# Attention, Sinkhorn routing and a mixture of experts on one core: the steps of the later token groups placed anew in time, some vector work given to GpSimd, the first routing rows loaded ahead

## The chip, the cores and the metric

The kernel runs on one core of a Trainium2 chip. The metric is the device time of one execution in microseconds (us), the median of three runs. A core has TensorE (PE, matrix products, which write into banks of PSUM), VectorE (DVE), ScalarE (ACT), GpSimd (POOL) and SyncE (SP, which here issues nearly all transfers between HBM and SBUF). Each engine works through its own list of instructions in order; semaphores make one wait for another.

## What is computed

For 2304 tokens of width 512, with x from an attention layer over 4 x 8 heads (its code is left out: the change does not touch it):

```python
def _moe_ref(x, w_gate, w1, w2):
    N, D = x.shape                      # 2304, 512
    E = w_gate.shape[1]                 # 8; w1 [8,512,1024], w2 [8,1024,512]
    logits = x @ w_gate
    P = np.exp(logits - logits.max())
    for _ in range(8):
        P /= P.sum(1, keepdims=True) + 1e-09
        P /= P.sum(0, keepdims=True) + 1e-09
        P *= N / E
    out = np.zeros((N, D), dtype=np.float32)
    for e in range(E):
        h = np.maximum(x @ w1[e], 0.0)
        ye = h @ w2[e]
        out += P[:, e:e + 1] * ye
    return out
```

Every expert is applied to every token, weighted by its routing column.

## The kernel before

After attention and routing, `experts()` works in three groups of 768 tokens. Group 0 is scheduled by loops. It also makes the split weights (a high part and the rest, `w1h`/`w1l`, `w2h`/`w2l`) and stores them in HBM (`cache`), from which groups 1 and 2 load them again. Both products of an expert use Strassen-like schemes with seven block products: one item is a quarter of an expert's hidden width, with 384 columns (half of the group) at a time.

Groups 1 and 2 take up the first item alone and then 15 pairs of items. Each step (a matmul group, an addition, a load) is entered with `at(t, f, key)` at a planned time, to which the table `SHIFT` adds a number for the step's key; then all steps are sorted by time and written out in that order. So the table sets the order on each engine; when a step runs is decided on the chip by its semaphores. The letter ahead of a key's colon names the unit: `1f`/`2f` the item alone, `k` and `m` the middle pairs of group 1 (even, odd), `o` and `n` those of group 2 (even, odd), seven of each, `1l`/`2l` the last pair. Whether a step that either engine can do goes to VectorE (0) or GpSimd (1) is read from the table `ON` by `who`.

In a unit, TensorE makes per item the seven first products (line 1567) into PSUM banks `s_4107` to `s_4113`, `f_4110`; their weights come through a ring of seven tiles (`w1h0`, `w1l0`, `w1h1`, `w1l1` of the names below), loaded by SP at line 1557. VectorE adds the banks up into `temps` and `raw` (line 1546); at line 1595 it applies the maximum with 0 and the routing weight, whose rows lie in two tiles `pb`, loaded at line 1763 (the second is the tile that held `wo`). ACT copies the high parts into `xh` and `hb` (line 1588), VectorE or GpSimd subtract for the low parts `xl`, `hb`. The combinations of quarters (`temps<-temps,f` and the like) are operands of the 28 sums (line 1688), which TensorE adds into banks and VectorE into the tiles `m`. Their weights are raw rows (line 1726) combined by ACT and GpSimd, and kept operands loaded at line 1751 (`w2h`, `w2l`, `wu`, `w1l0`). Between group 1's first item and its sums TensorE also makes the last second products of group 0 (line 854). At the end of a group the sums are transposed (line 1799) and added to the partial result `ydr` (loaded at line 1786, added at line 1807).

SP issues each transfer only when the one eight before it has landed. In its rows below, `DMAHW` names one of these eight, and `PE`, `Pool`, `DVE` the engines it waits for.

Of the kernel before, what the change touches and what calls it, by code (L numbers as in the profile page):

```python
# [17 lines left out]
def kernel(  # L18
# [872 lines left out]
    def experts():  # L891
# [324 lines left out]
        with tc.manual_schedule(engines={mybir.EngineType.Activation, mybir.EngineType.DVE}):  # L1216
            for q in range(NI):
# [30 lines left out]
                for f in pieces:  # L1248
# [4 lines left out]
                    n = len(late)  # L1253
# [57 lines left out]
        def open_late():  # L1311
# [587 lines left out]
        now = 0.0  # L1899
# [86 lines left out]
```

## Time and profile before

| | |
|---|---|
| three runs, median | 1741.79 us (1741.28 to 1742.5) |
| profiled execution | 1740.03 us |
| its span in the trace | 1738.2 us |
| TensorE busy | 1687.8 us (97%) |
| VectorE busy | 1400.4 us (81%) |
| GpSimd busy | 968.2 us (56%) |
| ACT busy | 695.7 us (40%) |

Groups 1 and 2 take the span from about 751 us to its end. TensorE is busy nearly all the time, so what can be saved without leaving out work is its waits. A busy share of TensorE also contains matmuls at the lower of its two clock levels (granted clock 0.50 is 1.2 GHz, 1.00 is 2.4 GHz).

### The profile page before, as it was taken

The numbers are of one execution on the slowest core, as the hardware profiler recorded it, in microseconds if no ns is written. First come the engines' busy times: TensorE is split into PE (matmuls) and PEld (weight loads), VectorE is DVE, ScalarE is ACT, GpSimd is POOL, SyncE is SP. The second block draws the span as 40 slices with busy tenths as digits, with TensorE's granted clock in tenths as the row PEclk, the third lists the DMA queues.
The fourth block names the chain that finished last, engine by engine and source line by source line (L and its number), as shares of the span: only waits on it lengthen the run. The fifth ranks groups of instructions, "written<-read, shape, count | busy, mean of one in ns | idle before, by whom it ended". The sixth has DMA issues, their size and how long they took to land.

```text
span 1738.2 us, 29930 instructions
## 1 busy us (share of the span) xinstructions
PE 1687.8 (97%) x9803; PEld 1556.7 (90%) x9803; DVE 1400.4 (81%) x2884; ACT 695.7 (40%) x1736; POOL 968.2 (56%) x1020
## 2 busy tenths in 40 slices
PE   7999999999999999989999999999899999999998
PEld 6777879889998889979999999999899999999997
DVE  8877747777777777767989889899988888787888
ACT  7877743333333343323333333333233333333331
POOL 5755544577777877755454555454544444444443
PEclk9999999999999999999999999999999999999999
DMA  5444334578888788597768777876676676675654
GB/s 136 100 108 110 86 116 143 187 228 262 271 269 266 242 269 266 187 297 245 266 218 305 223 260 230 272 244 211 212 238 224 188 242 209 193 245 185 227 187 152
DMA packets 311851, 370.23 MB, mean 213 GB/s; under 512 B 81280, under 2 KB 191120, under 8 KB 311696
## 3 DMA queue, kind: packets, MB, share of 16 engines
q1 hardware_dynamic: 309776, 367.49, 66.6%
q8 instruction: 79, 1.29, 0.3%
q10 hardware_dynamic: 1920, 0.82, 0.2%
q14 instruction: 76, 0.62, 0.1%
HBM read 260.59 MB, written 107.63 MB: 212 GB/s over the span
## 4 chain that ended last, share of the span: by engine, by line
PE 74%; DVE 17%; DMA 4%; issue 2%; ACT 1%; POOL 1%; SPq 0%; DVEq 0%; ACTq 0%; POOLq 0%
PE s L1688 15%; PE s L854 14%; PE s L1567 11%; PE s L1100 10%; DVE temps L1546 5%; PE f L1567 4%; PE f L1100 3%; PE sx L1688 3%; PE x L648 2%; DVE raw L1546 2%; DVE temps L1595 2%; PE s L408 2%; DVE xl L1546 2%; DVE m L1546 1%; PE s L489 1%
## 5 line engine op out<-in xcount | busy, mean ns | idle before, releaser
L1546 DVE TENSOR_TENSOR temps<-s,temps 128x384 f32<-128x384 f32 x270 | 144.9, 551 | 82.9 <-ACT w1h L1745 29.4
L1032 POOL TENSOR_TENSOR w1l<-raw,w1h 128x512 fp32r<-128x512 f32 x85 | 117.3, 1393 | 117.0 <-ACT w1h L1031 83.0
L1174 DVE SCALAR_TENSOR_TENSOR acc<-s,P,acc 128x512 f32<-128x512 f32 x168 | 123.0, 744 | 37.5 <-PE s L854 37.0
L854 PE MATMUL s<-w2h,hhh 128*128 128x512 f32 x372 | 147.0, 395 | 0.7 <-DVE acc L1174 0.7
L854 PE MATMUL s<-w2h,hhl 128*128 128x512 f32 x372 | 146.1, 393 | 0.0
L854 PE MATMUL s<-w2l,hhh 128*128 128x512 f32 x372 | 146.1, 393 | 0.0
L1546 DVE TENSOR_TENSOR m<-s,m 128x384 f32<-128x384 f32 x240 | 122.4, 549 | 11.8 <-PE s L1688 11.6
L1595 DVE SCALAR_TENSOR_TENSOR temps<-temps,pb 128x384 f32<-128x384 f32 x180 | 118.0, 672 | 8.6 <-DMA pb<-pd 7.6
L1588 ACT CAST xh<-temps 128x384 fp32r<-128x384 f32 x128 | 64.7, 513 | 140.5 <-DVE temps L1595 91.9
L1131 DVE TENSOR_TENSOR temps<-s,temps 128x384 f32<-128x384 f32 x132 | 71.6, 554 | 51.5 <-PE s L1100 36.4
L1567 PE MATMUL s<-xh,w1h 128*128 128x384 f32 x388 | 108.7, 335 | 0.0
L1567 PE MATMUL s<-th,w1l 128*128 128x384 f32 x364 | 104.5, 334 | 0.1
L1567 PE MATMUL s<-th,w1h 128*128 128x384 f32 x356 | 102.6, 335 | 0.1
L1065 POOL TENSOR_TENSOR w2l<-raw,w2h 128x512 fp32r<-128x512 f32 x62 | 98.0, 1598 | 2.0 <-ACT w2h L1064 2.0
L1688 PE MATMUL s<-hb,w1l 128*128 128x384 f32 x338 | 81.6, 337 | 5.2 <-ACT hb L1588 3.5
L854 PEld LDWEIGHTS s<-w2h,hhh 128*128 128x128 f32 x372 | 70.4, 189 | 17.8 <-DVE acc L1174 4.3
L854 PEld LDWEIGHTS s<-w2h,hhl 128*128 128x128 f32 x372 | 70.2, 189 | 15.0
L1546 POOL TENSOR_TENSOR xl<-raw,xh 128x384 fp32r<-128x384 f32 x39 | 44.3, 1137 | 68.8 <-ACT xh L1588 68.8
L854 PEld LDWEIGHTS s<-w2l,hhh 128*128 128x128 f32 x372 | 70.3, 189 | 13.6
L1084 ACT ACTIVATE hhh<-temps 128x384 fp32r<-128x384 f32 x100 | 52.5, 525 | 73.3 <-DVE temps L1131 71.6
L1085 DVE SCALAR_TENSOR_TENSOR hhl<-temps,hhh 128x384 fp32r<-128x384 f32 x100 | 81.0, 810 | 0.0
L1588 ACT CAST hb<-temps 128x384 fp32r<-128x384 f32 x90 | 44.8, 513 | 79.9 <-DVE temps L1595 75.7
(392 smaller groups left out, 5653.9 us busy)
## 6 DMA issues: line engine op xcount, KB each, us to landing
w1h<-cache SPq DMA_DIRECT2D x245, 256.0 KB
w1l<-cache SPq DMA_DIRECT2D x243, 256.0 KB
raw<-in_moe_w_dram SPq DMA_DIRECT2D x156, 256.0 KB
cache<-w1h SPq DMA_DIRECT2D x27, 896.0 KB
cache<-w1l SPq DMA_DIRECT2D x27, 896.0 KB
w2h<-cache SPq DMA_DIRECT2D x64, 256.0 KB
w2l<-cache SPq DMA_DIRECT2D x32, 256.0 KB
cache<-raw SPq DMA_DIRECT2D x32, 256.0 KB
```

The costliest lines, as they stand in the source:

```text
L854: nc.tensor.matmul(out=pt, lhsT=h_[:, f, cols], rhs=w[:, f], start=(n == 0), stop=(n == 5))
L1032: tt(out=wl[:, i:i + 2], in0=src, in1=f32(wh[:, i:i + 2]), op=ALU.subtract)
L1065: nc.gpsimd.tensor_tensor(out=wl[:, j], in0=raws[j], in1=f32(wh[:, j]), op=ALU.subtract)
L1085: late.append(lambda: nc.vector.scalar_tensor_tensor(out=hl[:, f, c], in0=src, scalar=0.0, in1=f32(hh[:, f, c]), op0=ALU.max, op1=ALU.subt ...
L1100: nc.tensor.matmul(out=pt[:, 0:HT], lhsT=w[:, wi, k], rhs=x[:, k], start=(n == 0), stop=(n == total - 1),)
L1131: nc.vector.tensor_tensor(out=o, in0=x, in1=y, op=ALU.add)
L1174: nc.vector.scalar_tensor_tensor(out=acc[:, j], in0=pt, scalar=P[:, t_, e:e + 1], in1=acc[:, j], op0=ALU.mult, op1=ALU.add,)
L1546: return lambda: eng.tensor_tensor(out=now_(o), in0=now_(x), in1=now_(y), op=op)
L1567: pe.matmul(out=bank[:, 0:HT], lhsT=w[:, a, k], rhs=x[b][:, k], start=bool(first and n == 0), stop=bool(last and n == 5),)
L1588: at(t, lambda: ac.copy(out=hop[j][n][0], in_=src), f"{n}H{j}")
L1595: at(t, lambda: dv.scalar_tensor_tensor(out=dst, in0=src, scalar=0.0, in1=pb[int(n[2]) - 1], op0=ALU.max, op1=ALU.mult), f"{n}F{j}")
L1688: pe.matmul(out=bank[n, a][:, 0:HT], lhsT=w[p][:, 128 * a:128 * a + 128], rhs=x[r], start=(j == js[0] and i == 0 and (n, a) not in held), ...
```

## The change

Three things change, all in `experts()` for groups 1 and 2. Every number of `SHIFT` is another one (780 keys, and a new one for the weight loads of group 1's first item, `"1f:wl": 3.078`), which orders the steps anew. Twenty-nine entries of `ON` are turned: 19 to GpSimd, 10 to VectorE. GpSimd's list grows from 949 to 974 rows, and its combinations `temps<-temps,f` from 7 to 28; VectorE's shrinks from 2425 to 2398. The routing rows of group 1's first item are entered 8.5 in place of 2 units of time ahead.

```diff
         SHIFT = {
-            "1f:E20": 1.795, "1f:E21": 1.394, "1f:E30": 0.066, "1f:E31": -0.556, "1f:E40": 0.241,
...
-            "k:t4L1": 0, "o:t4L1": 1, "k:t1S0": 1, "o:t1S0": 1, "k:t1S1": 0, "o:t1S1": 0,
+            "k:t4L1": 0, "o:t4L1": 0, "k:t1S0": 1, "o:t1S0": 1, "k:t1S1": 0, "o:t1S1": 1,
             "k:t2S0": 0, "o:t2S0": 0, "k:t2S1": 0, "o:t2S1": 0, "k:t3S0": 0, "o:t3S0": 0,
-            "k:t3S1": 0, "o:t3S1": 0, "k:t4S0": 0, "o:t4S0": 0, "k:t4S1": 0, "o:t4S1": 0,
-            "k:s1S0": 1, "o:s1S0": 1, "k:s1S1": 0, "o:s1S1": 0, "k:s2S0": 0, "o:s2S0": 0,
-            "k:s2S1": 0, "o:s2S1": 1, "k:s3S0": 0, "o:s3S0": 0, "k:s3S1": 0, "o:s3S1": 0,
+            "k:t3S1": 0, "o:t3S1": 0, "k:t4S0": 0, "o:t4S0": 1, "k:t4S1": 1, "o:t4S1": 1,
+            "k:s1S0": 0, "o:s1S0": 0, "k:s1S1": 1, "o:s1S1": 1, "k:s2S0": 0, "o:s2S0": 1,
+            "k:s2S1": 1, "o:s2S1": 1, "k:s3S0": 0, "o:s3S0": 0, "k:s3S1": 1, "o:s3S1": 1,
...
                 if items[0][1] == 0 or u == 0:
-                    pb_load(now - (2.0 if u == 0 else 10.0), g, items[0][0])
+                    pb_load(now - (8.5 if u == 0 and g == 1 else 2.0 if u == 0 else 10.0), g, items[0][0])
```

Two lines more stand in the table, so line 1546 of before is line 1548 after, and so on.

Three places show what moves. The first is SP's list in front of group 1's first products, before. `cache_3918` holds the split weights of the first products, `pd` the routing rows, and `in_moe_w2_dram` the raw rows of w2.

```order
L1557 DMA w1h1_3904<-cache_3918 128x512 [waits DMAHW1_49,PE_49]
L1557 DMA w1h1_3904<-cache_3918 128x512 [waits DMAHW2_49,PE_49]
L1005 DMA cache_3918<-wo_8303 128x512 [waits DMAHW3_49,Pool_49]
L1557 DMA w1h1_3904<-cache_3918 128x512 [waits DMAHW4_49]
L1557 DMA w1l1_3905<-cache_3918 128x512 [waits DMAHW5_49]
L1557 DMA w1l1_3905<-cache_3918 128x512 [waits DMAHW6_49,PE_49]
L1557 DMA w1l1_3905<-cache_3918 128x512 [waits DMAHW7_49]
L1037 DMA cache_3918<-w1h0_3902 128x7x256 [waits DMAHW0_49]
L1037 DMA cache_3918<-w1l0_3903 128x7x256 [waits DMAHW1_49]
L1557 DMA w1h0_3902<-cache_3918 128x512 [waits DMAHW2_49,DMAHW0_49,PE_49]
L1763 DMA pb_8326<-pd_97 128x3x128 [waits DMAHW3_49,DVE_49]
L1763 DMA pb_8327<-pd_97 128x3x128 [waits DMAHW4_49]
```

The same place after.

```order
L1005 DMA cache_3918<-wo_8303 128x512 [waits DMAHW1_49,Pool_49]
L1765 DMA pb_8326<-pd_97 128x3x128 [waits DMAHW2_49,DVE_49]
L1765 DMA pb_8327<-pd_97 128x3x128 [waits DMAHW3_49,DMAHW1_49]
L1037 DMA cache_3918<-w1h0_3902 128x7x256 [waits DMAHW4_49]
L1037 DMA cache_3918<-w1l0_3903 128x7x256 [waits DMAHW5_49]
L1559 DMA w1h1_3904<-cache_3918 128x512 [waits DMAHW6_49,PE_49]
L1559 DMA w1h1_3904<-cache_3918 128x512 [waits DMAHW7_49,PE_49]
L1559 DMA w1h1_3904<-cache_3918 128x512 [waits DMAHW0_49]
L1559 DMA w1l1_3905<-cache_3918 128x512
L1559 DMA w1l1_3905<-cache_3918 128x512 [waits DMAHW2_49,PE_49]
L1559 DMA w1l1_3905<-cache_3918 128x512 [waits DMAHW3_49]
L1559 DMA w1h0_3902<-cache_3918 128x512 [waits DMAHW4_49,PE_49]
```

The two loads of `pb` and the two stores of 7 x 256 columns stood behind the first six weight loads; now all seven weight loads stand behind them. The second `pb` load waits for lane DMAHW1, which is the store of `wo` from the tile that it overwrites.

The second place is VectorE's list in a middle pair of group 2 (an `o` pair), from the first to the last read of bank `s_4108`, before.

```order
L1546 TENSOR_TENSOR temps_4098<-s_4108,temps_4098 128x384
L1546 TENSOR_TENSOR temps_4098<-temps_4098,f2_8325 128x384
L1546 TENSOR_TENSOR temps_4098<-s_4109,temps_4098 128x384
L1546 TENSOR_TENSOR temps_4098<-f_4110,temps_4098 128x384
L1595 SCALAR_TENSOR_TENSOR temps_4098<-temps_4098,pb_8326 128x384
L1546 TENSOR_TENSOR raw_8323<-s_4107,temps_4098 128x384
L1546 TENSOR_TENSOR temps_4098<-s_4108,temps_4098 128x384
L1546 TENSOR_TENSOR xl_68<-raw_8324,xh_67 128x384
L1595 SCALAR_TENSOR_TENSOR temps_4098<-temps_4098,pb_8327 128x384
L1595 SCALAR_TENSOR_TENSOR raw_8323<-raw_8323,pb_8327 128x384
L1546 TENSOR_TENSOR xl_68<-temps_4098,xh_67 128x384
L1546 TENSOR_TENSOR temps_4098<-s_4108,temps_4098 128x384
```

After, from the same first read on.

```order
L1548 TENSOR_TENSOR temps_4098<-s_4108,temps_4098 128x384
L1597 SCALAR_TENSOR_TENSOR temps_4098<-temps_4098,pb_8326 128x384
L1548 TENSOR_TENSOR temps_4098<-s_4109,temps_4098 128x384
L1548 TENSOR_TENSOR xl_68<-raw_8324,xh_67 128x384
L1548 TENSOR_TENSOR temps_4098<-f_4110,temps_4098 128x384
L1548 TENSOR_TENSOR raw_8323<-s_4107,temps_4098 128x384
L1548 TENSOR_TENSOR temps_4098<-s_4108,temps_4098 128x384
L1597 SCALAR_TENSOR_TENSOR temps_4098<-temps_4098,pb_8327 128x384
L1597 SCALAR_TENSOR_TENSOR raw_8323<-raw_8323,pb_8327 128x384
L1548 TENSOR_TENSOR xl_68<-temps_4098,xh_67 128x384
L1548 TENSOR_TENSOR temps_4098<-s_4108,temps_4098 128x384
```

`temps<-temps,f2` has left for GpSimd, and the multiplication by `pb_8326` and the subtraction into `xl` have moved ahead of the addition out of bank `f_4110`.

The third place is SP's list in an `n` pair of group 2, before. `cache2` holds raw rows of w2, `cache3` kept operands.

```order
L1726 DMA raw2_8328<-cache2_3919 128x512 [waits DMAHW6_49,Pool_49]
L1726 DMA raw2_8329<-cache2_3919 128x512 [waits DMAHW7_49,Pool_49]
L1751 DMA wu_8496<-cache3_3920 128x512 [waits DMAHW0_49]
L1557 DMA w1l1_3905<-cache_3918 128x512 [waits DMAHW1_49,PE_49]
L1557 DMA w1l1_3905<-cache_3918 128x512 [waits DMAHW2_49,PE_49]
L1557 DMA w1l1_3905<-cache_3918 128x512 [waits DMAHW3_49,PE_49]
L1557 DMA w1h0_3902<-cache_3918 128x512 [waits DMAHW4_49,PE_49]
L1751 DMA w1l0_3903<-cache3_3920 128x512 [waits DMAHW5_49]
L1557 DMA w1h1_3904<-cache_3918 128x512 [waits DMAHW6_49,PE_49]
```

After.

```order
L1728 DMA raw2_8328<-cache2_3919 128x512 [waits DMAHW5_49,Pool_49]
L1728 DMA raw2_8329<-cache2_3919 128x512 [waits DMAHW6_49,Pool_49]
L1753 DMA w1l0_3903<-cache3_3920 128x512 [waits DMAHW7_49]
L1559 DMA w1h1_3904<-cache_3918 128x512 [waits DMAHW0_49,PE_49]
L1559 DMA w1h1_3904<-cache_3918 128x512 [waits DMAHW1_49,PE_49]
L1559 DMA w1l1_3905<-cache_3918 128x512 [waits DMAHW2_49,PE_49]
L1559 DMA w1l1_3905<-cache_3918 128x512 [waits DMAHW3_49,PE_49]
L1559 DMA w1l1_3905<-cache_3918 128x512 [waits DMAHW4_49,PE_49]
L1559 DMA w1h0_3902<-cache_3918 128x512 [waits DMAHW5_49,PE_49]
```

The load of the kept operand into `w1l0_3903` stood behind `wu` and four weight loads; now it follows the raw rows directly, ahead of six weight loads.

## Rows read from the trace of the kernel before

**Rows 1.** The page's busy us (share of the span), instructions.

```profile
PE 1687.8 (97%) x9803; PEld 1556.7 (90%) x9803; DVE 1400.4 (81%) x2884; ACT 695.7 (40%) x1736; POOL 968.2 (56%) x1020
```

**Rows 2.** TensorE's waits, 751 to 790 us: total, times, longest.

```profile
PE f L1567 <- DMA w1h<-cache: 3.5, 1, 3.5
PE s L1688 <- POOL xl L1546: 1.1, 1, 1.1
PE s L854 <- DVE acc L1174: 0.7, 1, 0.7
```

**Rows 3.** TensorE's waits, 790 to 1270 us.

```profile
PE s L1688 <- ACT xh L1588: 4.4, 1, 4.4
PE s L1688 <- DMA w2h<-cache: 2.6, 2, 2.4
...
PE s L1688 <- DVE temps L1546: 1.5, 1, 1.5
```

**Rows 4.** TensorE's waits, 1270 to 1710 us.

```profile
PE s L1688 <- DVE temps L1546: 5.5, 14, 0.6
PE s L1688 <- ACT hb L1588: 3.5, 3, 1.3
PE s L1688 <- DMA w1l<-cache: 1.7, 2, 1.1
```

**Rows 5.** Windows: busy us (x) of PE, PEld, DVE, ACT, POOL; clock, DMA share, GB/s.

```profile
761.00:767.00 6.00, 5.62 (x15) 4.85 (x16) 1.03 (x2) 0.62 (x3) 2.12 (x3) 0.50 0.77 129
801.00:805.00 4.00, 4.00 (x16) 4.00 (x15) 4.00 (x10) 2.52 (x5) 0.01 (x1) 0.57 0.56 182
805.00:820.00 15.00, 15.00 (x88) 15.00 (x87) 7.98 (x16) 2.97 (x7) 7.16 (x9) 1.00 0.64 173
1100.00:1200.00 100.00, 99.10 (x558) 95.96 (x557) 90.70 (x181) 34.06 (x80) 51.65 (x55) 1.00 0.78 261
1500.00:1600.00 100.00, 96.42 (x546) 94.16 (x546) 84.11 (x157) 33.04 (x79) 41.97 (x46) 1.00 0.65 205
```

**Rows 6.** The chain that ended last, 740 to 1738 us: start, us, what.

```profile
750.60 7.53 DMA cache<-w1h
...
795.02 5.21 DMA w2h<-cache
...
1249.25 7.32 DMA m<-ydr
...
1465.17 5.55 DMA w1l<-cache
```

**Rows 7.** SP's timeline, 742 to 763 us: start, us, transfer.

```profile
758.62 0.91 SPq L1763 DMA_DIRECT2D pb<-pd  x2
```

**Rows 8.** TensorE's timeline, 751 to 775 us, idle before in brackets.

```profile
751.32 0.44 PE L1567 MATMUL s<-xh,w1h 128*128 128x384 f32 x1
...
761.38 0.69 PE L1567 MATMUL f<-th,w1h 128*128 128x384 f32 x1 [3.52 <-DMA w1h<-cache]
...
774.32 0.51 PE L1688 MATMUL s<-xh,w1l 128*128 128x384 f32 x2
```

**Rows 9.** Transfers: 40 slices of 742 to 768 us; packets, 761 to 763.

```profile
GB/s 83 336 320 351 342 350 342 334 200 367 325 299 268 344 407 381 328 337 380 388 381 391 386 383 386 386 312 291 181 40 67 65 37 63 74 97 229 347 403 407
...
DMA packets 219, 0.11 MB, mean 55 GB/s; under 512 B 6, under 2 KB 219, under 8 KB 219
```

**Rows 10.** VectorE's timeline, 1433 to 1440 us.

```profile
1437.91 1.21 DVE L1546 TENSOR_TENSOR temps<-s,temps 128x384 f32<-128x384 f32 x2
```

**Rows 11.** Groups of VectorE and GpSimd, 1300 to 1700 us: busy, mean ns.

```profile
L1546 DVE TENSOR_TENSOR temps<-s,temps 128x384 f32<-128x384 f32 x120 | 64.5, 551 | 56.3 <-PE s L1567 23.4 <-ACT w1h L1745 23.3 <-ACT w1l L1745 4.2
L1595 DVE SCALAR_TENSOR_TENSOR temps<-temps,pb 128x384 f32<-128x384 f32 x79 | 56.8, 740 | 0.5
...
L1546 DVE TENSOR_TENSOR temps<-temps,f 128x384 f32<-128x384 f32 x20 | 18.7, 933 | 0.0
...
L1546 POOL TENSOR_TENSOR temps<-temps,f 128x384 f32<-128x384 f32 x6 | 8.1, 1353 | 35.1 <-DVE hb L1546 35.1
```

More of the change, by code (lines that the diff above doesn't have):

```diff
@@ L1334, in experts @@
         SHIFT = {
[170 rows of a table removed]
[171 rows of a table added]
+            "o:wl": 2.927,
         }
```

358 rows, old and new, of tables (ON, SHIFT) are left out of this document.

## The prediction

> **What bounds the kernel now.** I read the page's busy shares first: TensorE works 97% of the span [rows 1]. Then the waits of TensorE by stage, since only they can be won back, then the stretches by window, then for each wait the chain that leads to it. The change leaves the order as it was up to the queue in front of 751 us, so the search is in 751 to 1738 us.
>
> The waits fall into three kinds. At the start of group 1 TensorE stands 3.5 us for one weight load and 1.1 us for a GpSimd subtraction [rows 2]. In the rest of group 1 and the turn to group 2 it stands 4.4 us for an ACT copy, 2.6 us for weight loads and 1.5 us for VectorE [rows 3]. In group 2 it stands 10.7 us in 19 short waits (5.5 + 3.5 + 1.7) [rows 4]. The windows say the same: 99.1% busy in a steady stretch of group 1, 96.4% in one of group 2, where VectorE is busy only 84% [rows 5]. So group 2 is limited by order, not by an engine's total work. The windows show one more cost: the granted clock is 0.50 (1.2 GHz) in 761 to 767 us, right after the 3.5 us stand, and 0.57 in 801 to 805 us, after the one at 800 us. Full pace is 88 matmuls in 15 us, 0.17 each; the 16 in 801 to 805 us would need 2.7 of the 4.0 us, so that stand cost another 1.3 us.
>
> **The sum, place by place.** It is made against the profiled execution, 1740.03 us, which lies 1.76 us below the median of the three runs.
>
> *Start of group 1 (a cost).* Before, SP issues the loads of weights for six products, then the two stores of 896 KB from 750.60 us on [rows 6], then the load of the last product, then the routing rows `pb` at 758.62 us [rows 7]. TensorE starts the first product at 751.32 us and the seventh, which waits for that last load, at 761.38 us [rows 8]. Now the routing rows and the stores go ahead of all seven loads, as the order shows. Does a load overtake what was issued before it? The first store landed 7.53 us after its issue [rows 6], at 758.13 us, though both stores together are 4.8 us of transfer (below): the loads issued ahead of them took the time between. So transfers are served in the order of issue, and the first product waits for everything ahead: the raw rows and `wo` (about 750 us by the old issue times, an estimate), the routing rows, the stores. The stores hold 2 x 896 KB = 1.84 MB, at the 381 to 391 GB/s of the slices before 759 us [rows 9] 4.8 us. The routing rows hold 2 x 192 KB = 0.39 MB and run at 55 GB/s in 761 to 763 us [rows 9], which would be 7.1 us and is the bound above; the slices of that stretch reach from 37 to 97 GB/s, near 65 on most, which is 6.0 us. I take 6 us. The first load lands about 1.5 us behind the last store (256 KB at 385 GB/s is 0.7 us, and a landing). Sum: 750 + 6 + 4.8 + 1.5, about 762 us, for the first product, in place of 751.3.
>
> From there: before, 12.94 us passed from the seventh product's start to the sums at 774.32 us, with the cold clock and a 0.7 us wait for VectorE in it [rows 2, 8]. Now seven products follow the stand; the six more are 36 matmuls, at 0.17 each 6.1 us. The cold stretch stays, since TensorE stands longer than before, and the 0.7 us goes. 762 + 12.9 + 6.1 - 0.7 = 780.3 us, 6 us later. Against that the GpSimd wait behind it goes, 1.1 us [rows 2]. **+5 us.** Bounds: if the stores do not hold up the loads, the first product starts near 755 us and the old stand is gone, about -2 us; if the second half of the routing rows (its tile is `wo`'s, so it waits for the landing of `wo`, which the order shows) leaves the queue empty for 2 us and the rows take 7.1 us, about +9 us with the landings.
>
> *800 us.* The third `w2h` load was issued at 795.02 us and landed 5.21 us later [rows 6]; TensorE stood 2.4 us [rows 3] and paid 1.3 us of cold clock. That load now stands ahead of two weight loads, some 6 us earlier in the plan, and TensorE comes later. **-3.5 us**, at least -1, at most -3.7.
>
> *Around 836 us* VectorE's 1.5 us [rows 3]: its additions are ordered anew. **-1 us** (0 to -1.5).
>
> *Turn to group 2, 1259 us.* The chain: the last load of `ydr` took 7.32 us, to 1256.57 us [rows 6]; VectorE's additions waited for it, and behind them in its order stood the combination that ACT copies for TensorE's next sum: the 4.4 us [rows 3]. In the order the combination now goes ahead of one of the three additions that were before it, and two of the four loads are issued earlier, but the last one hardly. Behind so long a stand the clock will have fallen as at 800 us, at the same 1.3 us (an estimate from that row). I take half of the two: **-3 us** (0 to -5.7).
>
> *Group 2, per pair.* In the seven `o` pairs TensorE waits up to 0.6 us [rows 4] for a bank that VectorE reads last at 1437.91 us [rows 10]. In its order there stood ten operations between the first and the last read of that bank, now nine, and the one that left is `temps<-temps,f`, 933 ns on average here [rows 11]. 0.93 is more than 0.6, so this wait should close. In the `n` pairs, 1.7 us [rows 4] go to waits that end when `w1l0` lands: issued at 1465.17 us, 5.55 us on the way [rows 6]. It is now issued ahead of six loads, which the old issues put some 3 us earlier, more than the longest wait of 1.3 us. The three waits under ACT's name (3.5 us [rows 4]) stand at the same sum; ACT's copy was early, so I count them with it. All 10.7 us closed, less some that comes back: **-9 us** (-4 to -10.7).
>
> *What the moved operations cost.* 21 of these combinations go from VectorE (933 ns) to GpSimd (1353 ns [rows 11]): its list has 7 before and 28 now. GpSimd is busy 42% here, so I cost it at nothing; a result that is needed at once comes 0.42 us later, and if it stands behind another operation of that kind, up to 1.8 us. Additions that read a bank take 551 ns, multiplications with both inputs in SBUF 740 ns on average at the same place [rows 11]: two-input operations stretch. The Trainium skill's page "SBUF — State Buffer", section "Who interferes with whom", says that a VectorE instruction with two SBUF inputs contends with GpSimd's reads, and one with a single SBUF input does not. By that rule GpSimd work beside additions out of PSUM is free, and this part would be -10.7 in place of -9; the 933 and 740 ns against 551 agree with it, but where the new GpSimd work lies in time no row shows.
>
> Sum: 5 - 3.5 - 1 - 3 - 9 = -11.5 us; the end of the kernel changes by 0, within 3 us. On the profiled execution 1728.5 us, on the median 1741.8 - 11.5 = **1730.3 us**.
>
> **The rivals.** *The start costs nothing.* If loads pass stores, or the routing rows are quick when nothing competes, the start is -2 us and the sum -18.5: 1723.3 us. For it: the queue was full here before, so no row shows a load behind stores alone; against it: the routing rows ran at 55 GB/s in a stretch in which no packet of 2 KB or more moved [rows 9]. As a mechanism, these rows would have to move at the pace of the other transfers, 0.39 MB at 385 GB/s in 1.0 us, which takes 5 us off the start: 1725.3 us. The Trainium skill's page "DMA: Bandwidth & Descriptors", section "Specifications", gives 512 bytes as the least transfer for line rate, and a row of `pb` is cut into 128 x 4 = 512 bytes; by it this would be the case, but the row of 55 GB/s speaks against it, and the measurement decides.
>
> *The group-2 waits only move.* `temps` comes earlier, and then the next operand (`xl`, `hb`) is the late one. Then group 2 gives 2 us in place of 9 and the turn nothing: +5 - 3.5 - 1 - 2 = -1.5, 1740.3 us. For it: in each pair several operands come within some tenths of each other; against it: VectorE has 16% idle.
>
> *GpSimd comes late (slower).* Place: the pairs of both groups, at the 21 combinations that went to GpSimd. Each later by 0.42 us plus half of another such operation, 0.68 us, gives 1.1 us, 23 for the 21: -11.5 + 23 = +11.5, 1753.3 us. It decides from 11.5/21 = 0.55 us each. For it: the steady pairs of group 1 have no slack on TensorE to give (99.1% busy), only to lose. Against it: GpSimd is half idle.
>
> *The start is dear.* With +9 there and all else as forecast the sum is 9 - 3.5 - 1 - 3 - 9 = -7.5, 1734.3 us; with a third of the turn and 5 us of group 2, -1.5, 1740.3 us.
>
> **Chances and range.** The forecast, 1726 to 1736 us, 0.50; the start costs nothing, 0.12, of this 0.03 by the page's rule; the waits only move, 0.17; GpSimd late, 0.13; the start dear, 0.08. A difference of 0.2%, 3.5 us, is about what a measurement of this kernel can tell from no change. Faster: the first two, a third of the third (0.06) and most of the last (0.06), 0.74. Same: most of the third, 0.10, with 0.04 of the others. Slower: 0.12. The range from 1722 to 1742 us leaves out most of the GpSimd case and a little below, under 2 in 10; the forecast's own range is 1726 to 1736.
>
> **What would show it.** Right: `pb` issued near 750 us, the first product of group 1 near 762 us with a cold clock behind it, the sums 4 to 7 us later than 774.3; no stand at 800 and less at 1259; in group 2 the waits for `temps`, `hb` and `w1l` under 3 us in all, TensorE above 98.5% in its windows. Wrong: a first product before 757 us or after 765; waits of TensorE for GpSimd's `xl`, `hb` or for ACT copies of what GpSimd made, above 0.3 us in each pair; TensorE under 98.5% in 900 to 1200 us.

## The result and the profile after

The changed kernel takes 1710.53 us (median of four runs, 1710.07 to 1712.3) against 1741.53 us for the kernel before in the same runs: ratio 0.9827, 95% interval 0.981 to 0.9845. The forecast was 1730.3 us in a range from 1722 to 1742. The direction was right; the size was not: 31 us instead of 11.5. The spans of the two profiled executions, 1738.2 and 1708.3 us, differ by 29.9 us.

The page's first part for the changed kernel answers to [rows 1].

```profile
PE 1669.9 (98%) x9803; PEld 1555.8 (91%) x9803; DVE 1354.1 (79%) x2845; ACT 696.8 (41%) x1736; POOL 1004.3 (59%) x1059
```

TensorE has the same 9803 matmuls in both pages, while VectorE's busy time fell by 46 us and GpSimd's grew by 36. That says little about the place. For this I set the start of the same work in both traces side by side, since TensorE makes its products in the same order in both. These are TensorE's timelines at six places, first the kernel before: the first product of the first pair of group 1, of the next two pairs, of the item alone that opens group 2, of the first pair of group 2, and the sums of group 2's last pair.

```profile
783.11 0.33 PE L1567 MATMUL s<-xh,w1h 128*128 128x384 f32 x1
...
816.54 0.33 PE L1567 MATMUL s<-xh,w1h 128*128 128x384 f32 x1
...
848.40 0.33 PE L1567 MATMUL s<-xh,w1h 128*128 128x384 f32 x1
...
1244.48 0.33 PE L1567 MATMUL s<-xh,w1h 128*128 128x384 f32 x1
...
1267.76 0.33 PE L1567 MATMUL f<-xh,w1h 128*128 128x384 f32 x1
...
1710.40 0.51 PE L1688 MATMUL s<-xh,w2h 128*128 128x384 f32 x2
```

The same places in the changed kernel, with three rows of the start of group 1 ahead of them (they answer to [rows 8]).

```profile
754.40 0.50 PE L854 MATMUL s<-w2h,hhh 128*128 128x512 f32 x1 [3.70 <-DVE acc L1174]
...
761.88 0.69 PE L1569 MATMUL s<-xh,w1h 128*128 128x384 f32 x1 [5.19 <-DMA w1h<-cache]
...
779.17 0.51 PE L1690 MATMUL s<-xh,w1l 128*128 128x384 f32 x2
...
786.68 0.33 PE L1569 MATMUL s<-xh,w1h 128*128 128x384 f32 x1
...
817.30 0.33 PE L1569 MATMUL s<-xh,w1h 128*128 128x384 f32 x1
...
846.85 0.33 PE L1569 MATMUL s<-xh,w1h 128*128 128x384 f32 x1
...
1232.09 0.33 PE L1569 MATMUL s<-xh,w1h 128*128 128x384 f32 x1
...
1255.38 0.33 PE L1569 MATMUL f<-xh,w1h 128*128 128x384 f32 x1
...
1679.48 0.51 PE L1690 MATMUL s<-xh,w2h 128*128 128x384 f32 x2
```

The lead of the changed kernel grows from -3.57 us at the first pair (it is late there) to -0.76, 1.55, 12.39, 12.38 and 30.92 us. The differences from place to place are what each stage cost or gave (minus is time gained; the turn holds group 2's item alone, with its products and sums):

| stage | forecast, us | measured, us |
|---|---|---|
| start of group 1, up to its first pair | +5 | +3.6 |
| first pair (the stand at 800) | -3.5 | -2.8 |
| second pair (around 836) | -1 | -2.3 |
| the other pairs of group 1 | 0 | -10.8 |
| turn to group 2 | -3 | 0.0 |
| pairs of group 2, up to the last sums | -9 | -18.5 |
| end | 0 | +1.0 |
| sum | -11.5 | -29.9 |

The measured column is from one trace of each kernel. A second trace of the changed kernel, from a run described below (span 1711.5 us), gives 4.3, -3.0, -2.0, -8.7, 0.0, -17.6 and 0.3 us, so the two large terms hold to about 2 us.

Where the gain arose, TensorE's windows are nearly full. The view by window of the changed kernel, with the columns of [rows 5]:

```profile
755.00:765.00 10.00, 4.81 (x15) 3.94 (x14) 1.42 (x3) 2.00 (x5) 2.18 (x3) 0.51 1.06 384
900.00:1000.00 100.00, 100.00 (x577) 99.55 (x576) 85.58 (x173) 35.15 (x83) 56.40 (x66) 1.00 0.80 264
1100.00:1200.00 100.00, 99.23 (x565) 97.26 (x565) 88.23 (x178) 35.02 (x82) 56.63 (x64) 1.00 0.75 244
1500.00:1600.00 100.00, 100.00 (x577) 99.35 (x576) 82.71 (x161) 35.28 (x85) 55.18 (x58) 1.00 0.71 233
```

577 matmuls of 384 columns in 100 us are 0.173 us each, the full pace; in 1500 to 1600 us there were 546 before [rows 5]. Between 1270 and 1680 us TensorE has no listed wait any more, where [rows 4] had 10.7 us in 19. In 790 to 1270 us the waits of TensorE are these three and four of 0.4 to 0.6 us each:

```profile
PE s L1690 <- DVE m L1809: 2.3, 1, 2.3
PE s L1569 <- DVE tl L1548: 1.4, 1, 1.4
PE s L1569 <- DMA w1h<-cache: 0.7, 2, 0.4
```

### The profile page after: what moved, and what is told of

The parts are those of the page before. It is cut to its first block, busy times and chain, and to the rows that moved or that the text cites. A ratio compares the mean times of both kernels' runs of the same rounds, so it can differ in the third digit from the quotient of the medians.

```text
span 1708.3 us, 29942 instructions
## 1 busy us (share of the span) xinstructions
PE 1669.9 (98%) x9803; PEld 1555.8 (91%) x9803; DVE 1354.1 (79%) x2845; ACT 696.8 (41%) x1736; POOL 1004.3 (59%) x1059
## 4 chain that ended last, share of the span: by engine, by line
PE 88%; DVE 6%; DMA 3%; ACT 1%; issue 1%; POOL 1%; SPq 0%; DVEq 0%; ACTq 0%; POOLq 0%
PE s L1690 19%; PE s L1569 18%; PE s L854 15%; PE s L1100 10%; PE f L1569 6%; PE sx L1690 4%; PE f L1100 3%; PE x L648 2%; PE s L408 2%; PE f L1690 2%; DMA w1h<-cache 2%; PE s L489 1%; DVE m L1548 1%; PE f L854 1%; PE f L833 1%; DVE temps L1548 1%
## 5 line engine op out<-in xcount | busy, mean ns | idle before, releaser
L1548 POOL TENSOR_TENSOR xl<-temps,xh 128x384 fp32r<-128x384 f32 x46 | 57.2, 1243 | 92.9 <-ACT xh L1590 92.9
L1597 DVE SCALAR_TENSOR_TENSOR temps<-temps,pb 128x384 f32<-128x384 f32 x180 | 102.9, 579 | 1.2
```

Source lines behind the costliest of these rows:

```text
L1548: return lambda: eng.tensor_tensor(out=now_(o), in0=now_(x), in1=now_(y), op=op)
L1597: at(t, lambda: dv.scalar_tensor_tensor(out=dst, in0=src, scalar=0.0, in1=pb[int(n[2]) - 1], op0=ALU.max, op1=ALU.mult), f"{n}F{j}")
```

## The experiments

Two theories. Theory 1: the order of the steps (the times) decides, and TensorE's waits cost more than the idle time that was shown. Theory 2: the relief of VectorE (the engines' table) decides. On the start of group 1 a third question stood by itself: does the new queue order cost what the sum said?

**The two tables apart.** First the times alone, that is the changed kernel with all 29 turned entries of `ON` as before:

```diff
-            "k:t3S1": 0, "o:t3S1": 0, "k:t4S0": 0, "o:t4S0": 1, "k:t4S1": 1, "o:t4S1": 1,
+            "k:t3S1": 0, "o:t3S1": 0, "k:t4S0": 0, "o:t4S0": 0, "k:t4S1": 0, "o:t4S1": 0,
...
```

> All numbers of the time table and the routing rows as in the changed kernel, but the table of engines as before. If the order of steps decides (theory 1), it stays within 4 us of the changed kernel, under 1715 us. If the relief of VectorE by 29 moved entries decides (theory 2), it goes back by more than half of the 31 us, over 1726 us.

Measured: 1740.12 us, ratio 0.9991 to the kernel before (0.9978 to 1.0004). Then the engines alone, the kernel before with the changed `ON` and nothing else:

```diff
-            "k:t3S1": 0, "o:t3S1": 0, "k:t4S0": 0, "o:t4S0": 0, "k:t4S1": 0, "o:t4S1": 0,
+            "k:t3S1": 0, "o:t3S1": 0, "k:t4S0": 0, "o:t4S0": 1, "k:t4S1": 1, "o:t4S1": 1,
...
```

> The kernel before with only the table of engines of the changed one. Theory 1 (order decides): 1736 us or more, it may be slower than before, since the times were placed for the other engines. Theory 2 (relief of VectorE decides): 1726 us or less.

Measured: 1738.61 us, 0.9975 (0.9962 to 0.9989). Each theory was to keep more than half of the gain; neither table alone gives more than about a seventh of it. By stage, the new times alone start the first pair 3.2 us late, as the changed kernel does (3.6); they gain 3.3 us in group 1 from the third pair on and nothing in the pairs of group 2. The new engines alone gain 0.4 and 3.5 us there. The waits of TensorE in the pairs of group 2 (1275 to 1680 us) show why. With the new times and the old engines:

```profile
PE s L1690 <- DVE temps L1548: 6.1, 13, 0.8
PE s L1690 <- DVE hb L1548: 2.1, 6, 0.4
```

With the old times and the new engines:

```profile
PE s L1688 <- DVE xl L1546: 4.6, 7, 0.9
PE s L1688 <- DMA w1l<-cache: 2.8, 3, 1.4
PE s L1688 <- ACT hb L1588: 0.9, 2, 0.6
```

In the one, VectorE still does the work for which the new order leaves no room; in the other, the loads and the subtractions stand where they stood. So both theories fall as stated: the times are placed for these engines, and only the two together take the waits away.

**Two entries of the 29.** The changed kernel with the t4 combinations of the `o` pairs back on VectorE:

```diff
-            "k:t3S1": 0, "o:t3S1": 0, "k:t4S0": 0, "o:t4S0": 1, "k:t4S1": 1, "o:t4S1": 1,
+            "k:t3S1": 0, "o:t3S1": 0, "k:t4S0": 0, "o:t4S0": 0, "k:t4S1": 1, "o:t4S1": 0,
```

> The changed kernel with two entries put back to VectorE, the combinations t4 of both items in the o pairs of group 2 (14 operations). Theory 2: VectorE's last read of the bank comes 0.9 us later in each of seven pairs, the wait of about 0.6 us in front of the fifth sum returns, and with what such a wait costs in TensorE's pace the run is 4 to 7 us slower, 1715 to 1717 us. Theory 1: under 1 us, since the order alone left room.

Measured: 1723.39 us (ratio 0.9887, 0.9864 to 0.991), 12.9 us above the changed kernel's median, or 10.4 by the two ratios: well above the 4 to 7 us expected. From the first product of group 2's first pair to the sums of its last, the place where the two entries act, its trace takes 436.0 us and the changed kernel's 424.1. The waits of TensorE from 1270 to 1680 us and a window of it:

```profile
PE s L1690 <- DVE hb L1548: 6.4, 7, 0.9
PE s L1690 <- DVE temps L1548: 0.3, 2, 0.2
```

```profile
1300.00:1400.00 100.00, 97.86 (x556) 95.80 (x555) 83.25 (x161) 33.33 (x78) 43.28 (x46) 1.00 0.67 220
```

The waits shown are 6.7 us; the time lost in the pairs is 11.9. The window shows the same: 2.1 us idle, but 20 matmuls fewer than the 576 which the changed kernel has in 1300 to 1400 us, and 20 x 0.173 = 3.5 us. So the time lost is more than the idle time listed, here nearly twice as much.

**Four entries of group 1.**

```diff
-            "k:s1S0": 0, "o:s1S0": 0, "k:s1S1": 1, "o:s1S1": 1, "k:s2S0": 0, "o:s2S0": 1,
-            "k:s2S1": 1, "o:s2S1": 1, "k:s3S0": 0, "o:s3S0": 0, "k:s3S1": 1, "o:s3S1": 1,
-            "k:s4S0": 1, "o:s4S0": 1, "k:s4S1": 1, "o:s4S1": 0,
+            "k:s1S0": 0, "o:s1S0": 0, "k:s1S1": 0, "o:s1S1": 1, "k:s2S0": 0, "o:s2S0": 1,
+            "k:s2S1": 0, "o:s2S1": 1, "k:s3S0": 0, "o:s3S0": 0, "k:s3S1": 0, "o:s3S1": 1,
+            "k:s4S0": 1, "o:s4S0": 1, "k:s4S1": 0, "o:s4S1": 0,
```

> The changed kernel with four entries put back to VectorE: the raw sums s1 to s4 of the second item in the k pairs of group 1 (28 operations of 256 columns, about 0.4 us each). If the 10.8 us of group 1's steady pairs come from order that is fitted to these entries, each of seven pairs gets waits back: 1714 to 1722 us. If VectorE's 11% of idle time takes them up, under 1.5 us more than the changed kernel.

Measured: 1713.44 us (0.9837, 0.982 to 0.9854), 1.9 us above the changed kernel on the same chip (1711.55 us, below), between the two expectations and nearer the second; the intervals of the two ratios nearly coincide. From the third pair to the last of group 1 its trace takes 385.7 us, where the two traces of the changed kernel take 385.2 and 387.4. So VectorE takes these 28 operations up, and not every entry of the table matters as the two above do.

**The groups apart.** The kernel before with the changed numbers and engines of the units `2f`, `o`, `n` and `2l` alone, and the changed kernel with these as before. Some 400 entries of the tables differ in each; here is one line of the first:

```diff
...
-            "k:s2S1": 0, "o:s2S1": 1, "k:s3S0": 0, "o:s3S0": 0, "k:s3S1": 0, "o:s3S1": 0,
+            "k:s2S1": 0, "o:s2S1": 1, "k:s3S0": 0, "o:s3S0": 0, "k:s3S1": 0, "o:s3S1": 1,
...
```

> The kernel before with the times and engines of the changed one for the units of group 2 alone (2f, o, n, 2l). Aligned by unit, the two traces differ by 18.5 us between the first and the last sums of group 2. If these 18.5 us are group 2's own, this runs at 1742 - 18.5 = 1723 us, within 3; if they hang on what group 1 hands over, it stays above 1730 us.

> The changed kernel with the times and engines of group 2's units (2f, o, n, 2l) as before. Group 2 alone gave 20 us of 31. If the groups add up, this keeps 11 us: 1728 to 1733 us. If they lean on each other, the two parts miss the 31 us by more than 4.

Measured: 1721.4 us (0.9874, 0.9852 to 0.9896) and 1730.23 us (0.9942, 0.9923 to 0.9961). That is 20.1 and 11.4 us below the kernel before in the same runs, 31.5 together, and the whole change gave 31: the groups add up, and two thirds of the gain are group 2's own. The traces agree stage by stage. With group 2 alone changed, its pairs take 424.9 us (442.6 before, 424.1 changed) and group 1 from the third pair on 395.0 (396.1 and 385.2); with group 1 alone changed it is 442.8 and 384.8.

**The start of group 1.** The changed line alone, in the kernel before:

```diff
-                    pb_load(now - (2.0 if u == 0 else 10.0), g, items[0][0])
+                    pb_load(now - (8.5 if u == 0 and g == 1 else 2.0 if u == 0 else 10.0), g, items[0][0])
```

> The kernel before with the one changed line alone: the routing rows of group 1's first item go ahead of the two stores and the seventh weight load, behind the first six. By the reading that transfers are served in the order of issue, the seventh product comes about 6 us later, while VectorE no longer waits for the rows: 0 to 5 us slower than before, 1742 to 1747 us. If the rows were what holds group 1 up, it would be 2 to 5 us faster.

Measured: 1740.59 us, 0.9998 (0.9985 to 1.0011), no difference. The wait for the seventh load grew from 3.5 to 5.4 us and the seventh product came at 763.55 us, 2.2 us later and not the 6 expected; VectorE's 7.6 us for the rows went, and the first pair started at 782.42 us, 0.7 earlier than before. Now the other way, the changed kernel with that start put back (the line, and the key `"1f:wl"`):

```diff
-            "1f:w2s0": 0.678, "1f:wl": 3.078, "1l:E10": 2.027, "1l:E11": 1.565, "1l:E20": 2.032,
+            "1f:w2s0": 0.678, "1l:E10": 2.027, "1l:E11": 1.565, "1l:E20": 2.032, "1l:E21": 1.703,
...
-                    pb_load(now - (8.5 if u == 0 and g == 1 else 2.0 if u == 0 else 10.0), g, items[0][0])
+                    pb_load(now - (2.0 if u == 0 else 10.0), g, items[0][0])
```

> The changed kernel with the start of group 1 put back: routing rows entered 2 units ahead and no number for the weight loads of the first item, so that SP's list there reads as in the kernel before (six weight loads, the two stores, the seventh load, then the routing rows). If the new queue order costs what the trace shows (sums 4.85 us later), this runs 3 to 6 us below the changed kernel, near 1705 us, with the first product at 751 to 752 us. Rival: the early routing rows pay for themselves, because VectorE no longer stands 7.6 us for them and the next pairs catch up; then no gain, 1710 us or more, with waits of TensorE at 778 and 800 us back.

Measured: 1706.58 us (0.9792, 0.9768 to 0.9816), 4.0 us below the changed kernel's 1710.53, as expected. But the first product came at 756 us, not at 752. TensorE's timeline shows a new stand:

```profile
754.42 0.50 PE L854 MATMUL s<-w2h,hhh 128*128 128x512 f32 x1 [3.52 <-DVE acc L1174]
...
762.92 0.44 PE L1569 MATMUL s<-xh,w1l 128*128 128x384 f32 x1 [1.09 <-ACT temps L1632]
...
771.93 0.50 PE L854 MATMUL s<-w2h,hhh 128*128 128x512 f32 x1 [1.48 <-DVE acc L1174]
```

The changed kernel has the first of these stands too (3.70 us at 754.40 us, above), hidden there in front of the later one for the load. VectorE's list has a combination of raw rows (`raw<-raw,raw`, the key `1f:s4S0`, moved by -10.6 units) ahead of three additions out of PSUM, and it stood 5.7 us in front of it (5.85 in the changed kernel). I put this key back, in addition:

```diff
-            "1f:s4L0": 3.655, "1f:s4S0": -10.233, "1f:t1H0": 3.889, "1f:t1L0": 6.316,
+            "1f:s4L0": 3.655, "1f:s4S0": 0.406, "1f:t1H0": 3.889, "1f:t1L0": 6.316,
...
```

> The kernel with the start put back, and one key more: the combination s4 of the first item's raw rows at its old time. In the trace of the run before, VectorE stood 5.7 us in front of it with three additions out of PSUM behind it, and TensorE waited 3.5 us for these. If that order is the cause, the first product comes at 752 in place of 756.4 us, and the time is 1 to 3 us below that run: 1703.5 to 1705.5 us. Rival: the wait for the seventh load (3.5 us before) takes its place, less than 1 us.

Measured: 1706.73 us (0.9797, 0.9781 to 0.9813): no gain. The first product came at 752 us as expected, and then TensorE stood in front of a later one, for an ACT copy that frees its bank:

```profile
762.31 0.69 PE L1569 MATMUL s<-xh,w1l 128*128 128x384 f32 x1 [5.94 <-ACT temps L1632]
```

The chain of the same kernel shows what that copy stood behind:

```profile
751.96 9.19 DMA cache<-w1l
...
761.16 0.02 ACT w1l L1747
...
761.88 0.39 ACT temps L1632
...
762.31 4.21 PE s L1569 x12
```

ACT's list has the high part of a raw sum ahead of the copy; it goes into the tile `w1l`, whose contents are being stored, and that store lands 9.2 us after its issue. So the store was the next bound, and what was won ahead of the first product was lost again here: the sums start at 776.36 us, at 776.15 in the run before.

Next, in the same kernel, the store of the low parts is moved behind the routing rows. In this run ACT has begun to write the next operand into that tile when the store reads it, so part of what is stored is another operand; the transfers are of the same size.

```diff
...
-            at(-6.0, f, "held", 2)
+            at(-6.0, lambda f=f: f(ws=(0,)), "held", 1)
+            at(-1.5, lambda f=f: f(ws=(1,)), "held2", 1)
```

> The same, and the second of the two stores (the low parts) moved behind the routing rows, so that the seventh weight load and these rows stand behind one store only. If transfers are served in the order of issue, that load lands 2.4 us earlier (896 KB at 385 GB/s) and the wait of 3.5 us in front of the seventh product shrinks to about 1: 1701 to 1703.5 us. If the store's place does not matter, it runs as the kernel with one key more.

Measured: 1706.93 us (0.9803, 0.9785 to 0.982). ACT no longer waits for that store, but still for the one of the high parts ahead of it, to 758.42 us. TensorE's stand fell from 5.9 to 3.2 us; the end did not come sooner. Last, the whole old start (all keys of `1f` and the `pb` line as before), on one chip with the changed kernel again:

```diff
+            "1f:E20": 1.795, "1f:E21": 1.394, "1f:E30": 0.066, "1f:E31": -0.556, "1f:E40": 0.241,
...
-                    pb_load(now - (8.5 if u == 0 and g == 1 else 2.0 if u == 0 else 10.0), g, items[0][0])
+                    pb_load(now - (2.0 if u == 0 else 10.0), g, items[0][0])
```

> The changed kernel once more, on the chip of the three below, so that they can be told from it: 1709 to 1713 us.

> The changed kernel with every time of group 1's first item, and the routing rows, as before. The two runs with the start put back in part gained 4 us and then stuck on a wait that moved (VectorE, then an ACT copy out of a bank), since the other times of that item are placed for early routing rows. If that is so, the whole old start has only its own waits (3.5 us for the seventh load, 0.7 for VectorE, 1.1 for GpSimd) and runs with these two, 1705 to 1708 us. Rival: the rows of the next pair, placed for the new start, then come late, and it is no better than the changed kernel.

Measured: the changed kernel 1711.55 us (0.9828, 0.9811 to 0.9846), the old start 1707.3 us (0.9807, 0.9789 to 0.9825). The three kernels with an old start lie at 1706.6, 1706.7 and 1707.3 us: 4 us under the changed kernel, whichever of the waits in it they keep. In all three the first pair of group 1 starts at 783.1 to 783.8 us, 2.9 to 3.6 us ahead of the changed kernel's 786.68. The intervals of the ratios overlap with the changed kernel's, so 4 us is likely and not settled; all but one of the 13 runs of these three (1705.22 to 1707.46 and 1705.52 to 1710.63 us) lie below all eight of the changed kernel (1709.88 to 1713.26).

## Why the prediction was wrong, point by point

**The price of a wait (the step that failed).** The forecast took the idle time that the waits list: "All 10.7 us closed, less some that comes back: **-9 us**". All of them did close, and the pairs of group 2 gave 18.5 us. That idle time is too small a price can be seen at one of these waits. TensorE's timeline of the kernel before:

```profile
1437.57 0.34 PE L1688 MATMUL s<-xl,w1h 128*128 128x384 f32 x1
1438.52 0.62 PE L1688 MATMUL s<-xh,w1h 128*128 128x384 f32 x2 [0.61 <-DVE temps L1546]
1438.97 0.34 PE L1688 MATMUL s<-xl,w1h 128*128 128x384 f32 x1
```

The same four matmuls (the middle row stands for two) in the changed kernel:

```profile
1418.72 0.33 PE L1690 MATMUL s<-xl,w1h 128*128 128x384 f32 x1
1418.90 0.51 PE L1690 MATMUL s<-xh,w1h 128*128 128x384 f32 x2
1419.24 0.34 PE L1690 MATMUL s<-xl,w1h 128*128 128x384 f32 x1
```

One matmul is shown as 0.33 us long, but the next starts 0.17 us after it: they overlap (the profile models the ends; the starts carry the argument). From the first row to the third it is 1.40 us with the wait and 0.52 without, so 0.88 us are lost where 0.61 are listed. The wait is listed only from the end of the last matmul on, which hides 0.16 us of it, and the first two behind it take 0.11 us longer (0.62 in place of 0.51). A shorter delay is not listed at all, as here in group 1 of the kernel before, where the second row starts 0.46 us after the first and not 0.17:

```profile
1103.45 0.34 PE L1567 MATMUL s<-th,w1h 128*128 128x384 f32 x1
1103.91 0.62 PE L1688 MATMUL s<-xh,w2h 128*128 128x384 f32 x2
```

Taken from start to start in this way over all rows of the pairs of group 2, the kernel before loses 20.4 us against the full pace: 15.9 at the 19 waits of [rows 4], which list 10.7, 3.6 at 28 places where 0.06 to 0.31 us are missing and no wait is listed, and the rest in hundredths. The changed kernel loses 1.9, so 18.5 us were gained. The run with two entries turned back lists 6.7 us in nine waits; these cost 9.3 us, and with the delays that are not listed it lost 11.9 us more than the changed kernel does.

**"No slack on TensorE to give (99.1% busy), only to lose" (the same mistake).** The pairs of group 1 were costed at nothing, because their windows were 99.1% busy [rows 5]. They gave 10.8 us. Even of the listed waits in 790 to 1270 us, 1.9 us in seven short ones for VectorE's `wgp` had no term in the sum. The count of matmuls in the row had the answer: 558 in 100 us, where the full pace is 577 (the prediction itself took the pace from a count, 88 in 15 us, for the stretch at 800 us). 19 x 0.173 is 3.3 us in each 100, not 0.9. The whole stretches say the same. The windows from the third pair to the last of group 1, and over the pairs of group 2, in the kernel before:

```profile
848.00:1244.00 396.00, 391.56 (x2198) 379.13 (x2197) 356.87 (x700) 135.49 (x316) 201.43 (x217) 1.00 0.74 243
1268.00:1710.00 442.00, 430.94 (x2434) 419.86 (x2433) 368.85 (x683) 146.98 (x354) 194.62 (x215) 1.00 0.67 215
```

And in the changed kernel:

```profile
847.00:1232.00 385.00, 383.39 (x2197) 379.67 (x2196) 340.19 (x679) 134.81 (x314) 211.57 (x236) 1.00 0.76 249
1255.00:1679.00 424.00, 424.00 (x2438) 421.24 (x2437) 341.28 (x663) 147.66 (x354) 220.25 (x234) 1.00 0.69 224
```

The same work, to a few matmuls, takes 396 and 385 us, 442 and 424. Listed idle time fell by 2.8 us (4.4 to 1.6) where 11 were gained, and by 11.1 where 18 were. Worked out from the count, 396 - 2198 x 0.173 = 15.7 and 442 - 2434 x 0.173 = 20.9 us were there to be gained, and the rows of before would have said so. The second column of the same rows, the weight loads (PEld), says it too: their idle time fell from 16.9 to 5.3 us and from 22.1 to 2.8, close to what was gained. From start to start the gain in group 1 is 15.4 less 4.6 us: 6.8 before and 2.6 after at the listed waits, 7.5 (54 places) and 1.8 (17 places) where 0.06 to 0.30 us are missing and nothing is listed. So about half of what group 1 gave came from delays that no list of waits shows.

**The start, +5 us.** It cost 3.6, and by the steps forecast: `pb` at 749.3 us, the first product at 761.88 (762 forecast), a cold clock behind it (0.51 granted in 755 to 765 us), the sums at 779.17 us, 4.85 late, and the wait for GpSimd gone. From the first product to the sums it took 17.3 us where 18.3 were worked out, since the matmuls ran at the lower clock for some 3.4 us behind the stand and not for 5.5 as before. SP's timeline of the changed kernel shows the list, and the transfers in 40 slices from 749 to 760 us show it served in the order of issue:

```profile
748.88 0.33 SPq L1005 DMA_DIRECT2D cache<-wo  x1
749.30 2.55 SPq L1765 DMA_DIRECT2D pb<-pd  x2
751.90 0.48 SPq L1037 DMA_DIRECT2D cache<-w1h  x1
752.43 0.55 SPq L1037 DMA_DIRECT2D cache<-w1l  x1
753.08 3.97 SPq L1559 DMA_DIRECT2D w1h<-cache  x3
```

```profile
GB/s 201 372 350 216 380 283 145 153 58 30 73 65 9 47 74 69 82 82 110 110 121 112 250 266 326 378 395 380 395 380 387 384 384 384 387 387 387 387 391 387
```

The slow stretch from 751 to 755 us is `pb`, with both stores issued behind it; then the stores at 380 to 395 GB/s; then the load, landed at 761.84 us. The rows were through at 755.0 us, 1 us before the time worked out. One thing was luck: VectorE's stand of 5.85 us in front of a combination of raw rows, which the sum did not see, cost nothing because the load came later still. The wait for GpSimd, counted at 1.1 us, was worth 1.28.

**The rule of the Trainium skill on small transfers.** By "DMA: Bandwidth & Descriptors" (the Trainium skill), section "Specifications", 512 bytes is the least transfer for line rate. The rival had the rows done in 1.0 us. Here they ran at 9 to 121 GB/s in the slices of 751 to 755 us, with nothing but them moving, and the stores after them at 380 to 395. The measurement decides: that rival is out. But it does not follow that packets of 512 bytes are slow in themselves. The DMA engines were busy only 31, 21, 33 and 51% of these four microseconds (76% in 761 to 763 us of the kernel before, at 55 GB/s), and for some 0.3 us around 752.4 almost nothing moved: the second of the two loads, which waits for the store of `wo` to land (751.46 us), had just been issued. What holds the rows back is open.

**800 and 836 us.** -2.8 and -2.3 for -3.5 and -1: right in kind, off by 0.7 and 1.3 us. No stand is left at 800 us; two short waits for weight loads (0.62 and 0.29 us) came in near it.

**The turn to group 2, -3 us.** It gave nothing. TensorE's 4.4 us for the copy became 2.3 us for an addition behind the same kind of load (6.23 us for the last row of `ydr` in the chain, 7.32 before [rows 6]), and the cold clock stayed (0.50 granted in 1247 to 1249 us, as in 1260 to 1262 before). Half of the stand went, but a new wait came ahead of it, 1.4 us for VectorE's `tl` at 1236.40 us (in the list above), and the stretch as a whole took 23.3 us as before. The sum saw the wait that closed and not the one that opened.

**GpSimd late.** Out: GpSimd's combinations take 1316 ns in the changed kernel (1353 before [rows 11]), and no wait of TensorE is listed in the pairs of group 2. The groups of VectorE and GpSimd from 1275 to 1675 us:

```profile
L1597 DVE SCALAR_TENSOR_TENSOR temps<-temps,pb 128x384 f32<-128x384 f32 x81 | 47.0, 580 | 1.0
L1548 DVE TENSOR_TENSOR temps<-temps,f 128x384 f32<-128x384 f32 x6 | 3.3, 548 | 0.0
L1548 POOL TENSOR_TENSOR temps<-temps,f 128x384 f32<-128x384 f32 x21 | 27.6, 1316 | 46.8 <-ACT hb L1590 30.3 <-DVE hb L1548 16.6
```

Multiplications with both inputs in SBUF fell from 740 to 580 ns on average, the combinations left on VectorE from 933 to 548. By "SBUF — State Buffer" (the Trainium skill), section "Who interferes with whom", a VectorE instruction with two SBUF inputs contends with a GpSimd instruction that reads SBUF. The trace agrees: of the 41 multiplications (`temps<-temps,pb`) that have a row of their own in VectorE's timeline of the kernel before, 1300 to 1700 us, each of the 14 with no GpSimd instruction beside it took 0.55 us, and each of the 27 with one 0.72 to 1.23. The additions out of PSUM took 0.54 to 0.56 us either way. In the changed kernel 46 of the 81 multiplications have none beside them (0.55 us), and the other 35 took 0.62 on average. So GpSimd's work, though there is more of it, now lies less beside them. With the two entries turned back the multiplications stayed at 574 ns and the pairs still took 11.9 us longer, so shorter multiplications alone are not the gain.

**What stays open.** Which of the 23 entries that no run turned back by themselves matter; how the two tables depend on each other, beyond the waits shown above; why the old start in three forms reaches the first pair within 0.7 us whichever stand it keeps; and whether a start can be placed that keeps neither the load's wait nor the store's.

## What to carry to other kernels

Price a wait of a pipelined engine by the pace of the work around it, from the start of the last instruction before to the start of the first at full pace behind, and read the count of instructions in a window against the count at full pace (or the idle time of the weight loads), not its busy share. Where a table of times and a table of engines are changed together, neither can be costed alone: try them apart and together. Here each alone gave about a seventh or less of what both gave. A wait that is hidden behind a longer one comes out as soon as the longer one is taken away, so work out each stand's own end before counting on a fix.

## What the runs showed of the hardware that was not expected

TensorE's listed busy share can be 99.1% while 3.3% of its pace is missing (558 of 577 matmuls in 100 us). Loads of rows of 512 bytes ran at 9 to 121 GB/s with nothing else moving, under a third of what the stores behind them had on the same queue, and held up all that was issued behind them, though the DMA engines were busy only 21 to 51% of the time. One VectorE multiplication with both inputs in SBUF took 0.55 us whenever no GpSimd instruction ran beside it, and 0.72 to 1.23 us with one (41 rows of the kernel before); additions with one input in PSUM did not change.
